# Token loads of a 2:4-pruned matmul: two single tiles instead of a pair on SyncE, and one tile moved to ScalarE's queue

## The chip, the cores and the metric

The kernel runs on one core of a Trainium2 chip. The metric is the device time of one execution in microseconds (us); the number given for a kernel is the median of several runs. Tokens, weights, bias and output are bfloat16.

## The reference

```python
def reference(x, w, b):          # x (16, 512, 1024), w (1024, 1024), b (1024)
    B, S, D = x.shape
    N, M = 2, 4
    G = D // M
    wg = w.reshape(G, M, D)                      # groups of 4 consecutive rows
    mag = jnp.abs(wg)
    order = jnp.argsort(mag, 1)
    thr = jnp.take_along_axis(mag, order[:, M - N:M - N + 1, :], 1)
    mask = (mag >= thr).astype(w.dtype)          # the two largest of four are kept
    wp = (wg * mask).reshape(D, D)
    return jnp.einsum("bsd,df->bsf", x, wp) + b
```

In each column of the weights, of four consecutive rows the two with the larger magnitude are kept and the others are set to zero. Then 8192 tokens are multiplied with the pruned weights, and the bias is added.

## The kernel before

The 8192 tokens are 64 tiles of 128. The weights, 1024 by 1024, are held as four blocks `w_{g}_{h}`: g is the half of the rows, h the half of the columns. A partition of such a block holds four consecutive rows, so that one group of the pruning lies in one partition. The blocks are pruned in six pieces (line 61): four pieces of 256 columns for g = 0, numbers 0 to 3, and two of 512 for g = 1, numbers 4 and 5. `abs_piece` takes magnitudes, `prep_piece` finds the threshold of each group with maxima and minima on VectorE, then the mask (line 150) and the product with the weights (line 153). Piece 0 is done in smaller steps: its product comes first for rows 0 and 1 of the groups in two instructions, then for rows 2 and 3 in one.

TensorE contracts over partitions, so tokens must be transposed. The kernel has three ways:

- Tiles 0 to 7, first half of the contraction: they are loaded as they are (`load_x`, line 79, into tiles `xh`), transposed on TensorE (`transpose_half`, line 182, four 128x128 transposes per tile) into PSUM, and copied to SBUF by ScalarE (`copy_half`, line 187, into `xT`). The transposition gathers every fourth element, so that these tokens meet the weights in the layout in which they are pruned.
- Tiles 0 to 7, second half, and tiles 8 to 13 are loaded by transposing DMAs on SyncE's queue (`xg1`, line 324, and `xfill`, line 259).
- All later tiles are loaded by transposing DMAs, two tiles and then eight at a time (`issue_batch`, line 271).

For all but the first kind the pruned weights are needed in the order of rows; four DMAs per block bring them there (`unpack`, line 172, into `wp_nat`).

In front, the order of the work is written out by hand as a list of short words (`FRONT`, line 285). `W` and `w` are matmuls on constants with which TensorE is kept running until tokens come (line 105); `T.t` transposes tile t; `C.t` copies it; `N.i.t.m` and `M.i.t` multiply tile t with piece i (line 203; 256 columns for pieces 0 to 3); `A` and `P` prune a piece; `U` unpacks; `X` and `Y` are the matmuls of tiles 8 to 13. The words around the change read:

```python
W W W W W W W W W w w T.0 T.1 C.0 T.2 T.3 C.1 w T.4 C.2 N.0.0.0 N.0.0.1
N.0.1.0 N.0.1.1 T.5 N.0.2.0 N.0.2.1 N.0.0.2 N.0.0.3 ...
```

Every engine runs its own instructions in this order and waits at each one for what it needs. The loads stand ahead of this list (lines 83 to 91): each is issued on SyncE's queue or, if `nc.scalar` is named, on ScalarE's. All DMAs of the program, of both queues, take turns on eight completion semaphores; a DMA's issue waits until the one that stands eight places before it has landed.

After the front, TensorE takes one tile after another with 16 matmuls of 512 columns (line 371), VectorE adds the bias (line 248) into a tile `o_pair` that holds the outputs of two tiles, and ScalarE's queue stores it. Pair p holds tiles 2p and 2p + 1; a pair named in `singly` (line 214) is stored in two DMAs, one per tile (lines 221 and 224), the others in one (line 228). There are five such buffers.

Of the kernel before, what the change touches and what calls it, by code (L numbers as in the profile page):

```python
# [10 lines left out]
def kernel(  # L11
# [7 lines left out]
    nc = tc.nc  # L19
# [49 lines left out]
    def load_w(g, c0, c1, eng=nc.sync, m0=0, m1=4):  # L69
        dst = w_gh[(g, c0 // FH)][:, m0:m1, c0 % FH:c0 % FH + c1 - c0]  # L70
        K(eng.dma_start(dst, wv[:, g, m0:m1, c0:c1]))  # L71
# [4 lines left out]
    def load_x(ta, tb, eng=nc.sync):  # L76
        xt = const.tile([P, tb - ta, KH], bf16, name=f"xh_{ta}")
        src = xf[ta * P:tb * P, 0:KH].rearrange("(t p) c -> p t c", p=P)
        K(eng.dma_start(xt[:], src))
        for t in range(ta, tb):  # L80
            xh[t] = xt[:, t - ta, :]

    load_w(0, 0, 256, nc.sync, 0, 2)
    load_w(0, 0, 256, nc.scalar, 2, 4)
    load_x(0, 2)
    load_x(2, 4, nc.scalar)
    load_x(4, 5)
    load_x(5, 6)
    load_w(0, 256, 512)
    load_x(6, 8)  # L90
    load_w(0, 512, 1024)
# [119 lines left out]
            o_left[t // 2] = 2 if t == NT - 2 else 4  # L211
        return o_pair[t // 2][:, t % 2, :]

    singly = range(10, 17)

    def half_done(t):
        p = t // 2
# [188 lines left out]
```

## Time and profile before

| | |
|---|---|
| median of 3 runs | 233.23 us (232.80 to 233.49) |
| the profiled execution's own time | 233.29 us |
| its span in the trace | 231.5 us |
| TensorE busy | 226.3 us, 98% of the span |
| VectorE busy | 120.2 us |
| ScalarE busy | 18.0 us |
| DMA, mean over the span | 165 GB/s |
| first matmul on tokens (a transposition) starts | 5.24 us |
| first matmul with pruned weights starts | 6.44 us |

Times within the trace count from the start of the span. In the profile, PE is TensorE's matmuls and PEld its loading of the stationary operand, DVE is VectorE, ACT is ScalarE, POOL is GpSimd; SPq and ACTq are the instruction queues of SyncE and ScalarE that issue DMAs. A line of the order of time gives the start, the length, engine, source line, operation, output and input, and the number of instructions merged into it; in brackets stands how long the engine was idle before, and what ended that. The length of an issue on SPq or ACTq is the time that the queue needed for it, not the transfer; a transfer's landing is told separately, as the time from issue to landing.

Loads ahead of the front, in their order on each queue, as the trace has them:

| queue | what | size | issued at | issue to landing |
|---|---|---|---|---|
| SyncE | piece 0, rows 0 and 1 of the groups | 128 KB | 0.73 | 2.8 |
| SyncE | tiles 0 and 1 | 256 KB | 1.24 | 4.0 |
| SyncE | tile 4 | 128 KB | 1.75 | 4.2 |
| SyncE | tile 5 | 128 KB | 2.25 | 4.1 |
| SyncE | piece 1 | 256 KB | 2.72 | 4.5 |
| SyncE | tiles 6 and 7 | 256 KB | 3.44 | 4.5 |
| SyncE | pieces 2 and 3 (w_0_1) | 512 KB | 4.09 | 5.9 |
| SyncE | piece 4 (w_1_0) | 512 KB | 4.70 | 6.7 |
| ScalarE | piece 0, rows 2 and 3 of the groups | 128 KB | 0.73 | 3.0 |
| ScalarE | tiles 2 and 3 | 256 KB | 1.25 | 4.4 |

### The profile page before, as it was taken

Reading aid. Unit: us, or ns where it says so; the run is one execution under the profiler, and the core shown is the slowest. Engines: PE = TensorE matmul, PEld = TensorE weight load, DVE = VectorE, ACT = ScalarE, POOL = GpSimd, SP = SyncE. Lnnn points to the kernel's source line nnn. Section 1 sums busy time; section 2 is a strip of 40 time slices with the busy share of each in tenths; the row PEclk is TensorE's granted clock in tenths of the full one; section 3 lists DMA queues with packets and bytes.
Section 4 is the critical chain, followed back from the end, with each engine's and each line's share of the span. In section 5 each row is a group of like instructions: output and inputs, shape, how many; then the busy total and the mean of one; then the engine's idle time right before and its main releaser. Section 6 shows DMA issues by size and latency. Waiting matters only on the chain.

```text
span 231.5 us, 2773 instructions
## 1 busy us (share of the span) xinstructions
PE 226.3 (98%) x1137; PEld 110.5 (48%) x1156; DVE 120.2 (52%) x213; ACT 18.0 (8%) x33; POOL 0.7 (0%) x6
## 2 busy tenths in 40 slices
PE   7999999999999999999999999999999999999995
PEld 3887444444444444444444444444444444444443
DVE  3999887867997324424424424423423433433434
ACT  2867500000000000000000000000000000000000
POOL 1000000000000000000000000000000000000000
PEclk9999999999999999999999999999999999999999
DMA  6999889999647222991249622595128921122222
GB/s 196 295 193 270 192 177 184 267 252 307 258 181 272 91 95 65 233 290 55 84 120 265 159 95 91 131 258 179 69 91 210 316 108 40 53 91 91 91 93 91
DMA packets 77100, 38.19 MB, mean 165 GB/s; under 512 B 63136, under 2 KB 68896, under 8 KB 77088
## 3 DMA queue, kind: packets, MB, share of 16 engines
q1 hardware_dynamic: 67712, 20.91, 42.0%
q10 hardware_dynamic: 9376, 17.11, 20.0%
q8 instruction: 9, 0.15, 0.3%
q14 instruction: 3, 0.02, 0.0%
HBM read 3.41 MB, written 16.78 MB: 87 GB/s over the span
## 4 chain that ended last, share of the span: by engine, by line
PE 96%; DMA 2%; issue 1%; DVE 0%; SPq 0%
PE bank L371 73%; PE bank L203 17%; PE bank L263 6%; DMA xh<-in_x_dram 2%; PE bank L182 1%; DVE o_last L354 0%; SPq L71 0%; PE bank L105 0%
## 5 line engine op out<-in xcount | busy, mean ns | idle before, releaser
L371 PE MATMUL bank<-wp_nat,xTb 128*128 128x512 bf16 x737 | 161.7, 379 | 0.8
L248 DVE TENSOR_TENSOR o_pair<-bank,bias_sb 128x512 bf16<-128x512 f32 x104 | 67.3, 687 | 99.5 <-PE bank L371 94.2
L371 PEld LDWEIGHTS <-xTb 128*128 128x128 bf16 x752 | 73.6, 98 | 88.7
L239 DVE TENSOR_TENSOR stage<-bank,stage 128x512 f32<-128x512 f32 x22 | 14.2, 687 | 4.1 <-PE bank L203 4.1
L203 PE MATMUL bank<-w,xT 128*128 128x256 bf16 x128 | 14.7, 273 | 0.0
L243 DVE TENSOR_TENSOR o_pair<-stage,bias_sb 128x512 bf16<-128x512 f32 x22 | 14.0, 683 | 0.0
L203 PE MATMUL bank<-wp_nat,xg 128*128 128x512 bf16 x62 | 13.9, 379 | 0.1
L203 PEld LDWEIGHTS <-xT 128*128 128x128 bf16 x128 | 12.2, 98 | 1.8 <-ACT xT L187 0.3
L235 ACT COPY stage<-bank 128x512 f32<-128x512 f32 x22 | 11.5, 613 | 4.5 <-PE bank L203 4.5
L203 PE MATMUL bank<-wp_nat,xfill 128*128 128x512 bf16 x47 | 10.6, 379 | 0.1
L263 PE MATMUL bank<-wp_nat,xfill 128*128 128x512 bf16 x47 | 10.5, 379 | 0.1
L203 PEld LDWEIGHTS <-xg 128*128 128x128 bf16 x64 | 6.3, 98 | 7.6
L263 PEld LDWEIGHTS <-xfill 128*128 128x128 bf16 x48 | 4.7, 98 | 5.7
L203 PEld LDWEIGHTS <-xfill 128*128 128x128 bf16 x48 | 4.7, 98 | 5.5
L371 PE MATMUL bank<-wp_nat,xTs 128*128 128x512 bf16 x32 | 7.1, 379 | 0.0
L150 DVE TENSOR_TENSOR mask<-mag,thr 128x512 bf16<-128x512 bf16 (+3 forms) x10 | 5.6, 581 | 0.2
L153 DVE TENSOR_TENSOR w<-w,mask 128x512 bf16<-128x512 bf16 (+3 forms) x10 | 5.6, 580 | 0.1
L371 PEld LDWEIGHTS <-xTs 128*128 128x128 bf16 x32 | 3.1, 98 | 3.8
L105 PE MATMUL bank<-const-bfloat16-1.0 128*128 128x512 bf16 (+1 forms) x12 | 4.0, 493 | 0.8 <-PEq L390 0.8
L187 ACT COPY xT<-bank 128x512 bf16<-128x512 bf16 x8 | 4.1, 605 | 3.0 <-PE bank L182 3.0
L120 DVE TENSOR_SCALAR mag<-w 128x512 uint16<-128x512 uint16 (+2 forms) x6 | 2.7, 466 | 2.8 <-DMA w<-in_w_dram 2.7
L263 PE MATMUL bank<-wp_nat,xTb 128*128 128x64 bf16 (+3 forms) x40 | 3.7, 251 | 0.0
(20 smaller groups left out, 26.1 us busy)
## 6 DMA issues: line engine op xcount, KB each, us to landing
out_dram<-o_pair ACTq DMA_DIRECT2D x24, 512.0 KB, 2.8
out_dram<-o_pair ACTq DMA_DIRECT2D x15, 256.0 KB, 2.0
wp_nat<-w SPq DMA_DIRECT2D x16, 128.0 KB, 2.8
w<-in_w_dram SPq DMA_DIRECT2D x3, 512.0 KB, 5.9
xh<-in_x_dram SPq DMA_DIRECT2D x2, 256.0 KB, 4.2
xh<-in_x_dram ACTq DMA_DIRECT2D x1, 256.0 KB, 4.4
xh<-in_x_dram SPq DMA_DIRECT2D x2, 128.0 KB, 4.2
w<-in_w_dram SPq DMA_DIRECT2D x1, 256.0 KB, 4.5
```

The costliest lines, as they stand in the source:

```text
L105: K(nc.tensor.matmul(bank[7][:, :n], lhsT=ones[:, :P], rhs=ones[:, :n], start=True, stop=True))
L120: K(nc.vector.tensor_single_scalar(mag[:, ms].bitcast(u16), w_of(i)[:, ms].bitcast(u16), 0x7FFF, op=Alu.bitwise_and))
L150: K(nc.vector.tensor_tensor(mask[:, ms, c], mag[:, ms, c], tb, op=Alu.is_ge))
L153: K(nc.vector.tensor_tensor(w_of(i)[:, ms, c], w_of(i)[:, ms, c], mask[:, ms, c], op=Alu.mult))
L187: K(nc.scalar.copy(xt[:], src))
L203: K(nc.tensor.matmul(dst, lhsT=lhs, rhs=rhs, start=c0 == 0 and m == 0, stop=c1 == FH and m == 3))
L235: K(nc.scalar.copy(stage[(h, t)][:], bank[own[(h, t)]][:]))
L239: K(nc.vector.tensor_tensor(st, bank[own[(2 + h, t)]][:], st, op=Alu.add))
L243: K(nc.vector.tensor_tensor(get_o(t)[:, f], stage.pop((h, t))[:], bias_sb[:, f], op=Alu.add))
L248: K(nc.vector.tensor_tensor(get_o(t)[:, f], bank[bk][:], bias_sb[:, f], op=Alu.add))
L263: K(nc.tensor.matmul(bank[bk][:, :c1 - c0], lhsT=xN[t][:, kt, :], rhs=wp_nat[h][:, kt, c0:c1], start=kt == 0, stop=kt == KT - 1))
L371: K(nc.tensor.matmul(bank[bks[h]][:], lhsT=xN[t][:, kt, :], rhs=wp_nat[h][:, kt, :], start=kt == 0, stop=kt == KT - 1))
```

## The change

Tiles 0 and 1 are loaded by one DMA each, both on SyncE's queue, where one DMA brought both. Tile 5 goes from SyncE's queue to ScalarE's, behind tiles 2 and 3. SyncE's queue holds, in this order, the first half of piece 0, tile 0, tile 1, tile 4, piece 1, tiles 6 and 7, and the rest as before. There is one DMA more ahead of the front, so that each later DMA is one place further on in the turn of the eight semaphores. Pair 10, tiles 20 and 21, is no longer in `singly` and is stored by one DMA, so that from there on the turn is as before. The instructions of TensorE, VectorE and GpSimd and their order are the same; on TensorE the first transposition of tile 1 has a wait of its own for its tokens.

```diff
     load_w(0, 0, 256, nc.sync, 0, 2)
     load_w(0, 0, 256, nc.scalar, 2, 4)
-    load_x(0, 2)
+    load_x(0, 1)
     load_x(2, 4, nc.scalar)
+    load_x(1, 2)
+    load_x(5, 6, nc.scalar)
     load_x(4, 5)
-    load_x(5, 6)
     load_w(0, 256, 512)
     load_x(6, 8)
     load_w(0, 512, 1024)
...
-    singly = range(10, 17)
+    singly = range(11, 17)
```

## The prediction

> **What bounds the kernel now.** I read the page's busy shares first, then the chain that ended last, then the order of time of the first 10 us, then SyncE's queue. The profiled execution took 233.29 us, of which 231.5 us are its span; 1.79 us lie around it. The median of the three runs is 233.23 us, so a difference found in the trace is carried over to the median as it is.
>
> ```profile
> PE 226.3 (98%) x1137; PEld 110.5 (48%) x1156; DVE 120.2 (52%) x213; ACT 18.0 (8%) x33; POOL 0.7 (0%) x6
> ```
>
> TensorE is busy for 226.3 of 231.5 us, so only idle TensorE time can be won, and there is little of it. The chain, in order of time (start, length, what), says where:
>
> ```profile
> 1.24 3.96 DMA xh<-in_x_dram
> 5.20 0.05 issue
> 5.24 1.08 PE bank L182 x16
> ...
> 9.46 13.11 PE bank L203 x115
> 22.57 0.05 issue
> 22.62 10.74 PE bank L203 x49
> ```
>
> Up to 5.20 us the end hangs on the first transfer of tokens (tiles 0 and 1, 256 KB, issued at 1.24). From 5.24 on it is TensorE alone; the 0.05 us pieces later on are no wait that the profile can name. So the change can act only in the head. There, in order of time:
>
> ```profile
> 0.77 3.75 PE L105 MATMUL bank<-const-bfloat16-1.0 128*128 128x512 bf16 x11 [0.77 <-PEq L390]
> ...
> 5.24 1.08 PE L182 MATMUL bank<-ident,xh 128*128 128x128 bf16 x16 [0.72 <-DMA xh<-in_x_dram]
> ...
> 5.69 3.04 ACT L187 COPY xT<-bank 128x512 bf16<-128x512 bf16 x6 [2.41 <-PE bank L182]
> 5.88 0.48 DVE L153 TENSOR_TENSOR w<-w,mask 128x256 bf16<-128x256 bf16 x2
> ...
> 6.44 0.77 PE L203 MATMUL bank<-w,xT 128*128 128x256 bf16 x4
> 6.73 0.42 DVE L153 TENSOR_TENSOR w<-w,mask 128x512 bf16<-128x512 bf16 x1
> 6.82 0.11 PEld L203 LDWEIGHTS <-xT 128*128 128x128 bf16 x2 [0.28 <-ACT xT L187]
> ...
> 7.31 1.70 PE L203 MATMUL bank<-w,xT 128*128 128x256 bf16 x14
> ```
>
> The reader is to see four things. TensorE idles 0.72 us (4.52 to 5.24) for the tokens. The first real matmul (6.44) needs the first pruned half of piece 0, and VectorE delivers that at 5.88 + 0.48 = 6.36. The matmuls of tile 1 start at 6.82 because ScalarE's copy of tile 1 ends only then: ScalarE copies one tile every (3.04 - 0.60) / 5 = 0.49 us, and its first copy starts at 5.69. Tile 2's start at 7.31 for the same reason. And the copies begin late only because tile 0's tokens do.
>
> **The change, part by part.**
>
> *Steps of TensorE.* Transposes follow each other by (1.08 - 0.22) / 15 = 0.057 us, so one tile of four takes 0.23; the 256-column matmuls by (1.70 - 0.27) / 13 = 0.11. From a release to the next start I take 0.05 (landing 5.20, start 5.24).
>
> *Tile 0's landing.* Not in the trace as a transfer of 128 KB in the first place. Bounds: at best its half of the pair's bytes is saved at the whole rate of its queue's share. Between 4.5 and 5.24 us the sixteen engines moved about 381 GB/s, two queues at work, so 131 KB at half of that are 0.69 us and at all of it 0.34 us: landing at 4.51 to 4.86; at worst it lands with the pair, at 5.20. I take 4.5, because ScalarE's pair is in flight beside it (landed 1.25 + 4.4 = 5.6). Its four transposes then start at 4.55, right after the warm-up, and ScalarE's first copy at about 4.97 instead of 5.69. Everything up to 5.04 gives the same sum, see the copies below.
>
> *Tile 1's landing.* It has the same bytes ahead of it on its queue as the end of the pair had, so 5.20; the late bound is the slot that it takes over, issued at 1.75, from which tile 4's tokens took 4.2 us: 5.95 to 6.0. I take 5.20, the row of the same bytes. Its transposes run from 5.24, the last ends at 5.63, and its copy starts at 5.66 instead of 6.18.
>
> *Tiles 2 and 3* keep their place (second on ScalarE's queue, landing 5.6): transposes 5.66 to 6.11. One filler matmul, 0.06.
>
> *Tile 4 and tile 5.* Tile 4 stays third of SyncE's token transfers, tile 5 goes to ScalarE's queue. Before, they landed at 5.98 and at 2.25 + 4.1 = 6.38. Now they come side by side: tile 4 at 5.58 at the whole rate of 347 GB/s (window 5.24 to 6.44) counted from 5.20, 5.95 at half, 6.33 at a third; I take 5.95. It is needed at 6.17, so up to 0.1 costs nothing and the late bound costs 0.2. Tile 5 at half rate after 5.62 lands at 6.4 and is needed at 6.85: nothing. The Trainium skill, "DMA: Bandwidth & Descriptors", section "Issuing engines are not separate DMA queues", says that transfers from two engines share the same 16 DMA engines and interleave; it speaks against any gain from spreading, and by it the half-rate figure is the right one, while separate queues would give 5.58. No start on TensorE depends on which.
>
> *First matmul.* Tile 4's transposes end their issue at 6.17 + 0.23 = 6.40, VectorE's half is there at 6.36 + 0.05 = 6.41: first matmul at 6.41 instead of 6.44. Here the next thing that is late shows itself: **VectorE's pruning**. From there two matmuls of tile 0, two of tile 1 (copy done at 5.66 + 0.59 = 6.25, no wait any more), four transposes of tile 5, two matmuls of tile 2 (copy 6.15 to 6.75, no wait): 0.22 + 0.22 + 0.23 + 0.22 = 0.89, so the third matmul of tile 0 starts at 7.30. VectorE's second half is there at 6.73 + 0.42 + 0.05 = 7.20: no wait. Before, that matmul started at 7.31 + 2 x 0.11 = 7.53. **The gain is 0.23 us**, made up of the two waits on ScalarE (0.16 at 6.82, where 6.66 was the next step, and 0.04 at 7.31) and 0.03 at the first matmul. Of the 0.72 us of idle time the rest is only moved, to wait for VectorE. All of it won would be 7.53 - 7.20 = 0.33; more isn't there while VectorE starts at 3.58 with the weights, which the change doesn't touch.
>
> *Is it carried to the end?* Piece 1 is needed by TensorE 14 matmuls after 9.30, at 10.85, now 10.62; VectorE has its first half at 9.94 + 0.42 = 10.36. Slack 0.2 us, and 256 KB of piece 1's weights have the same bytes ahead on their queue. Later pieces have more (pruned at 13.69, used at 14.3). After that no wait stands on TensorE, so the shift reaches the end.
>
> *A new wait on SyncE.* Transfers take turns on eight completion semaphores, and the issue of one waits until the one eight places before it has landed. One more transfer up front moves all later ones by a place. The row that shows such a wait now:
>
> ```profile
> SPq L259 <- DMA xh<-in_x_dram: 0.3, 1, 0.3
> ```
>
> Here the transposing load of xfill waited for tiles 2 and 3 (5.6). After the change it is the transfer before it, the weights of w_1_0, that waits for them: issued at 5.65 instead of 4.70, with 0.63 us of issuing; xfill follows at 6.3 instead of 5.63. Tiles 6 and 7 wait for the first weights (3.55 against an issue at 3.44: 0.1). Behind that on SyncE's queue, each later by 0.7 us at most:
>
> ```profile
> 5.63 6.48 SPq L259 DMA_TRANSPOSE xfill<-in_x_dram  x1
> 12.25 3.50 SPq L172 DMA_DIRECT2D wp_nat<-w  x4
> 15.79 0.62 SPq L71 DMA_DIRECT2D w<-in_w_dram  x1
> 16.46 5.22 SPq L324 DMA_TRANSPOSE xg<-in_x_dram  x1
> 22.48 2.49 SPq L172 DMA_DIRECT2D wp_nat<-w  x4
> ```
>
> Their users: xfill landed at 15.8 and the four unpacks by 17.9, used from 21.2; the last weights at 20.0, used by VectorE at 22.37; xg at 23.8, used at 26.3; the unpacks of 22.48 wait for VectorE's pruning (21.23 + 1.23 = 22.46) and not for the queue, which is free at 21.7, then 22.4. These have the smallest slack: 0.8 us of queue, and 1.2 more from landing (22.48 + 2.6) to use (26.5, now 26.3), 2.0 against 0.7. Cost nothing; without that cover it would be the lateness beyond it, one for one.
>
> *ScalarE's third issue* (0.5 us, row of 1.25) pushes its table load from 1.79 to 2.3, done at 3.8 with the small copy; the first copy is at 4.97. Nothing.
>
> *Output.* Tiles 20 and 21 leave in one store of 512 KB at 84.8 instead of two of 256 KB at 81.34 and 84.79: one issue of 0.35 us less on an idle ScalarE, landing 0.8 later (2.8 against 2.0 us), its buffer used again only five pairs on. Nothing.
>
> Sum: 233.29 - 0.23 = 233.06 against the profiled time, **233.00 us** against the median.
>
> **The rivals.**
>
> 1. *Landing follows the slot, not the bytes.* Then tile 1 lands at 6.0. Transposes of tile 1 at 6.04, tiles 2 and 3, filler and tile 4 behind them (0.95 in all): first matmul at 6.99, third of tile 0 at 6.99 + 0.89 = 7.88 against 7.53: slower by 0.35, 233.6. Decisive from a landing at 5.65 on, where the gain is used up. For it: five SyncE transfers in a row took 4.0 to 4.5 us from issue to landing whatever their size. Against it: DMA engines moved 381 GB/s then, so bytes and not slots were the limit. The Trainium skill, the same page, section "Rules for kernel authors", tells to merge small transfers because each has a fixed cost; by that rule splitting loses.
>
> 2. *Tile 0 isn't earlier.* If the queues share out so that it lands with the old pair (after 5.04), copies start as before and only the 0.03 is left: 233.2. For it: the pair of 256 KB took 4.0 us from its issue and the 128 KB behind it 4.2, so size hardly shows. Against it: those 128 KB were queued behind the pair.
>
> 3. *SyncE's queue becomes the bound.* Only if lateness exceeds 2.0 us; the two xfill loads took 6.48 and 3.29 us to issue for the same size, so 3.2 us of scatter exist, but the longer one is already in the chain. With 3.2 beyond the 0.7, TensorE would wait 1.9 us, less the gain: 1.7 slower, 234.9.
>
> 4. *More than my sum.* Bounded by VectorE at 0.33: 232.9. Over 0.7 us only by something that the profile doesn't show.
>
> **How the numbers follow.** Forecast 0.62 (232.9 to 233.1), rival 2 0.14, rival 1 0.13, rival 3 0.03, rival 4 0.08 (half of it beyond 0.7 us). Within 0.3% (0.70 us), about what a measurement of this kernel can tell from no change, lie the forecast, rival 2 and most of rival 1. The three runs of before scatter from 0.43 below to 0.26 above their median, which puts a few hundredths of each at the bounds: faster 0.09, same 0.83, slower 0.08. The range takes 232.80 - 0.33 = 232.5 below and rival 1 above, 233.6.
>
> **What would show it.** Right: tile 0's transposes start by 4.9; the first matmul at 6.41, directly after VectorE; no wait on ScalarE at tiles 1 and 2; third matmul of tile 0 at 7.30; w_1_0 issued at 5.65; no gap on TensorE at 21 to 27 us. Wrong: tile 1 after 5.65, or a gap on TensorE before tile 4's transposes or tile 5's, or at xfill or xg.

## The result and the profile after

The changed kernel takes 234.58 us, the median of 17 runs (233.55 to 236.29); the kernel before took 233.19 in 17 runs beside them (232.80 to 233.76). The ratio is 1.0069, 95% interval 1.0049 to 1.0088: slower by 1.6 us (the medians lie 1.4 us apart), where 0.2 us of gain were forecast. The profiled execution of after took 233.55 us and is the fastest of its 17; 7 of the 17 took 235.5 us or more.

Busy times are those of before within 0.1 us. From the page of after:

```profile
PE 226.2 (98%) x1137; PEld 110.6 (48%) x1156; DVE 120.2 (52%) x213; ACT 18.1 (8%) x33; POOL 0.7 (0%) x6
```

So the work is the same and the difference is idle time of TensorE. The chain that ended last (start, length, what) says for what:

```profile
1.75 4.16 DMA xh<-in_x_dram
5.95 0.86 PE bank L183 x12
6.81 0.06 PE bank L106
6.87 0.22 PE bank L183 x4
7.09 0.44 PE bank L204 x4
7.53 0.22 PE bank L183 x4
7.75 1.53 PE bank L204 x14
9.28 0.45 PE bank L183 x8
9.72 13.11 PE bank L204 x115
```

Before, the end hung on the tokens issued at 1.24, which landed at 5.20. Now it hangs on the next transfer of the same queue: tile 1, issued at 1.75, landed at 5.90. The way from there to the block of 115 matmuls is shorter than it was: 3.77 us from 5.95 to 9.72, against 4.22 from 5.24 to 9.46. Four transposes, those of tile 0, are already done (0.22 us), and the matmuls that waited for ScalarE's copies no longer wait. In before these two pieces of the chain were:

```profile
6.61 0.61 PE bank L203 x4
...
7.44 1.58 PE bank L203 x14
```

They took 0.44 and 1.53 in after. So 0.71 us were lost at the start and 0.45 won behind it. The 0.26 us that are left are the whole difference between the two profiled executions (233.55 and 233.29). The order of time shows the new wait (in brackets the idle time before, and what ended it):

```profile
0.77 3.87 PE L106 MATMUL bank<-const-bfloat16-1.0 128*128 128x512 bf16 x11 [0.77 <-PEq L391]
...
4.48 0.38 PE L183 MATMUL bank<-ident,xh 128*128 128x128 bf16 x4
...
4.90 0.59 ACT L188 COPY xT<-bank 128x512 bf16<-128x512 bf16 x1 [1.09 <-PE bank L183]
...
5.93 0.49 DVE L154 TENSOR_TENSOR w<-w,mask 128x256 bf16<-128x256 bf16 x2
...
5.95 0.86 PE L183 MATMUL bank<-ident,xh 128*128 128x128 bf16 x12 [1.09 <-DMA xh<-in_x_dram]
...
6.93 0.60 PE L204 MATMUL bank<-w,xT 128*128 128x256 bf16 x4
```

Tile 0 is transposed at 4.48, right after the warm-up, and ScalarE copies it at 4.90. Then TensorE has nothing for 1.09 us until tile 1 has landed. VectorE has the first pruned half at 5.93 + 0.49 = 6.42, but the first matmul starts at 6.93: it isn't VectorE that is late, it is the transposes, which stand ahead of it in TensorE's order. In the waits of after, TensorE has no other wait for data in the whole execution:

```profile
PE bank L183 <- DMA xh<-in_x_dram: 1.1, 1, 1.1
```

That accounts for 233.55. It doesn't yet account for 234.58, the median, nor for the seven runs from 235.5 on.

### The profile page after: what moved, and what is told of

It reads as the page before. It is cut to its first block, busy times and chain, and to the rows that moved or that the text cites. A ratio compares the mean times of both kernels' runs of the same rounds, so it can differ in the third digit from the quotient of the medians.

```text
span 231.8 us, 2771 instructions
## 1 busy us (share of the span) xinstructions
PE 226.2 (98%) x1137; PEld 110.6 (48%) x1156; DVE 120.2 (52%) x213; ACT 18.1 (8%) x33; POOL 0.7 (0%) x6
## 4 chain that ended last, share of the span: by engine, by line
PE 95%; DMA 2%; issue 1%; DVE 0%; SPq 0%
PE bank L372 73%; PE bank L204 16%; PE bank L264 6%; DMA xh<-in_x_dram 2%; PE bank L183 1%; DVE o_last L355 0%; SPq L71 0%; SPq L79 0%; PE bank L106 0%
```

## The experiments

Two questions were open. Why does tile 1 land at 5.90 and not at 5.20? And what makes other runs longer than the profiled one? For the first the theories were: the bytes (what is served ahead, on both queues, sets the landing), the place (the issue slot sets it, whatever the bytes: a queue supplies the engines with one transfer per issue), and short transfers as such, with single DMA engines that come late. For the second: a still later landing, or TensorE's pace after a longer idle time.

A transfer counts as landed when sixteen completions are in. They are taken here as one for each of the sixteen DMA engines, though the trace names no engine. Where landings are told below, they are read from the trace: first, twelfth and last of the sixteen.

### Which part of the change costs

**e1_split_only**: the changed kernel, with tile 5 left on SyncE's queue.

```diff
-    load_x(5, 6, nc.scalar)
     load_x(4, 5)
+    load_x(5, 6)
```

> Only the split of tiles 0 and 1 is done; tile 5 stays on SyncE's queue behind tile 4. Theory of turns (the DMA engines serve one transfer of SyncE's queue, then one of ScalarE's, and so on, so tile 1 stands behind the 256 KB of tiles 2 and 3): the split alone is what delays tile 1, which lands at about 5.9 as in the changed kernel, with tile 4 next at about 6.2 and tile 5 at 6.6; the first matmul with weights starts at about 6.9, the third of tile 0 at 7.8 against 7.53 before. Rival, contention with tile 5 on ScalarE's queue delays tile 1: then tile 1 lands at 5.2 here and the time is 233.0. Time by turns: 233.5 at the least, and as far up as 236 in some runs if the longer idle time of TensorE brings its clock down.

**e2_move_only**: the kernel before, with only tile 5 moved to ScalarE's queue.

```diff
     load_x(0, 2)
     load_x(2, 4, nc.scalar)
+    load_x(5, 6, nc.scalar)
     load_x(4, 5)
-    load_x(5, 6)
```

> Only tile 5 goes to ScalarE's queue, tiles 0 and 1 stay one transfer of 256 KB. If the split alone is the cause (as the run with the split alone suggests: 234.2 with tile 5 on SyncE's queue), nothing changes: tiles 0 and 1 land at 4.6 to 5.2, time 233.2 within 0.2. Rival, the move is a cause of its own (short transfers on two queues at once hold some of the 16 DMA engines up): tile 4 or tile 5 lands after 6.5 and TensorE waits for it; 233.5 or more.

Measured: the split alone 234.20 (233.63 to 234.64, 7 runs; before 233.21), ratio 1.0039 [1.0025, 1.0052], tile 1 landed at 5.99. The move alone 233.21 (232.96 to 234.05, 10 runs; before 233.11), ratio 1.0004 [0.9993, 1.0015]. The split costs; moving tile 5 costs nothing that can be measured. On the chip of e1_split_only the whole change cost no more than the split alone (e7_after_again, below: 1.0031).

### The place in the queue, or the bytes

**e17_third_slot**: the kernel before, with the pair of tiles kept, but SyncE's half of piece 0 in two transfers of 64 KB. The pair has the same bytes ahead of it and is third instead of second.

```diff
-    load_w(0, 0, 256, nc.sync, 0, 2)
+    load_w(0, 0, 256, nc.sync, 0, 1)
+    load_w(0, 0, 256, nc.sync, 1, 2)
...
-    singly = range(10, 17)
+    singly = range(11, 17)
```

> Before, with SyncE's half of piece 0 in two transfers of 64 KB: tiles 0 and 1 stay one transfer of 256 KB with the same bytes ahead of it, but it is the third in SyncE's order, issued at about 1.75 instead of 1.24. If the landing goes by the place in the queue and its issue, the pair lands where the third transfer lands elsewhere, 5.5 to 6.8 us (in before 5.98); the third matmul of tile 0 comes that much later than at 7.53, 0.3 to 1.6, so 233.5 to 234.8 us, and longer where TensorE loses its pace. If it goes by the bytes ahead, the pair lands at 4.6 to 5.2 as in before, and the time is 233.0 to 233.4 us. If short transfers as such make some engines late, the last of the sixteen completions comes 0.7 us or more behind the twelfth; else within 0.4 us as in before.

Measured: 235.29 us (234.36 to 236.12, 6 runs; before 233.12), ratio 1.0086 [1.0060, 1.0111]. The chain of e17_third_slot begins:

```profile
1.18 0.42 SPq L71
1.65 4.46 DMA xh<-in_x_dram
6.15 1.90 PE bank L183 x16
```

The pair, whole and with no byte more ahead of it on its queue, was issued at 1.65 and landed at 6.10. In before it landed at 5.20, in e2_move_only, e4_less_warm and e10_no_warm, where it is second too, at 4.58 to 5.02. So the bytes ahead on its own queue, by which it had to come at 4.6 to 5.2, don't set the landing. But it isn't the start that is late. The first completion came at 4.58 (4.67 in before), the twelfth at 5.44 (4.94), the last at 6.10: the spread grew from 0.53 to 1.52 us. The last came 0.66 us behind the twelfth, between the two bounds that the expectation had set for short transfers as such. And the other queue isn't held fixed: ScalarE's tiles 2 and 3, which had landed behind the pair in before (5.62), landed ahead of it here (5.16). The lengths show a second loss, taken up further down: sixteen transposes took 1.90 us where before took 1.08.

**e18_act_short_first**: the changed kernel, with ScalarE's queue in the order tile 5, then tiles 2 and 3, so that half as many bytes are served between tile 0 and tile 1.

```diff
-    load_x(2, 4, nc.scalar)
+    load_x(5, 6, nc.scalar)
     load_x(1, 2)
-    load_x(5, 6, nc.scalar)
+    load_x(2, 4, nc.scalar)
```

> The changed kernel with ScalarE's queue in the order tile 5, then tiles 2 and 3: tile 1 keeps its place and issue (third on SyncE, 1.75), but the transfer that the queues serve between tile 0 and tile 1 has 128 KB instead of 256. If tile 1 is late because of the bytes served in between, its first completions come at about 4.4 instead of 4.75 and its last by 5.3; tiles 2 and 3 come last, at 5.6 to 6.0, and the time is 233.2 to 233.8 us. If it is late by its place in the queue, its last completion stays at 5.9 to 6.7 and the time is 234.0 to 235.

Measured: 234.75 us (234.68 to 236.50, 4 runs; before 233.12), ratio 1.0089 [1.0054, 1.0124]. Tile 1's first completion came at 4.61 instead of 4.75, its last at 6.31; tiles 2 and 3 landed only at 7.33, and TensorE waited for both. What the DMA engines did meanwhile is shown by stretches of 0.5 us. A line holds each engine's busy time, then the granted clock, the DMA share (the mean busy share of the sixteen DMA engines; overlapping packets can bring it over 1) and GB/s. In e18_act_short_first:

```profile
4.00:4.50 0.50, 0.50 (x2) 0.15 (x1) 0.50 (x3) 0.00 (x0) 0.00 (x0) 1.00 0.23 59
4.50:5.00 0.50, 0.50 (x6) 0.43 (x5) 0.50 (x4) 0.00 (x0) 0.00 (x0) 1.00 0.63 223
```

The same stretches of before, where the pair and tiles 2 and 3, 512 KB, filled them:

```profile
4.00:4.50 0.50, 0.50 (x4) 0.20 (x2) 0.50 (x4) 0.00 (x0) 0.00 (x0) 1.00 1.02 361
4.50:5.00 0.50, 0.03 (x1) 0.00 (x0) 0.50 (x3) 0.00 (x0) 0.00 (x0) 1.00 1.09 381
```

And those of after:

```profile
4.00:4.50 0.50, 0.50 (x5) 0.24 (x4) 0.50 (x4) 0.00 (x0) 0.00 (x0) 1.00 1.13 256
4.50:5.00 0.50, 0.36 (x7) 0.20 (x4) 0.50 (x4) 0.10 (x1) 0.00 (x0) 1.00 0.73 248
```

And the first of them in e5_act_singles (further down), where tiles 2 and 3 are split too:

```profile
4.00:4.50 0.50, 0.50 (x2) 0.15 (x1) 0.50 (x3) 0.24 (x2) 0.00 (x0) 1.00 1.05 373
```

The last two columns are to be read. In e18_act_short_first hardly a byte moved at 4.0 to 4.5 us. Tile 1 had been issued at 1.75 and tile 4 at 2.21, and all ahead of them had landed by 4.34. A reading that fits is that the engines had nothing to work on yet: an issue of 128 KB (1.75 to 2.21, 0.46 us) takes SyncE about as long as one of 256 KB (1.24 to 1.75, 0.51 us in before), so that two short transfers give the engines in two slots what one pair gives them in one. At 4.0 to 4.5 us eleven of the thirteen profiles with tiles 0 and 1 split moved 59 to 320 GB/s, and the four that have the pair where before has it (before, e2_move_only, e4_less_warm, e10_no_warm) moved 346 to 381. But the reading isn't shown. In after the share was 1.13 while 256 GB/s were moved: the engines were busy, and some packets took long, up to 0.89 us where most took 0.05. And e5_act_singles, which has the most short transfers in front, moved 373.

**The same question from other sides.** Each is the changed kernel with one edit; e5_act_singles, e12_pool, e13_w_sp_split and e14_w_sp_pair shift `singly` by the DMA that they add or take away, as the change does.

```diff
e6_x1_act: tile 1 on ScalarE's queue, tiles 2 and 3 third on SyncE's
-    load_x(2, 4, nc.scalar)
-    load_x(1, 2)
+    load_x(1, 2, nc.scalar)
+    load_x(2, 4)

e5_act_singles: tiles 2 and 3 in two transfers too
-    load_x(2, 4, nc.scalar)
+    load_x(2, 3, nc.scalar)
     load_x(1, 2)
+    load_x(3, 4, nc.scalar)

e8_one_queue: all tokens on SyncE's queue
-    load_x(2, 4, nc.scalar)
     load_x(1, 2)
-    load_x(5, 6, nc.scalar)
+    load_x(2, 4)
     load_x(4, 5)
+    load_x(5, 6)

e11_w_on_act: SyncE starts with tile 0
-    load_w(0, 0, 256, nc.sync, 0, 2)
+    load_w(0, 0, 256, nc.scalar, 0, 2)

e12_pool: tile 1 issued by GpSimd
-    load_x(1, 2)
+    load_x(1, 2, nc.gpsimd)

e13_w_sp_split: piece 0 whole on SyncE, ScalarE starts with tiles 2 and 3
-    load_w(0, 0, 256, nc.sync, 0, 2)
-    load_w(0, 0, 256, nc.scalar, 2, 4)
+    load_w(0, 0, 256)

e14_w_sp_pair: as e13_w_sp_split, with tiles 0 and 1 in one transfer again
-    load_x(0, 1)
+    load_x(0, 2)
     load_x(2, 4, nc.scalar)
-    load_x(1, 2)
```

> Tile 1 alone goes to ScalarE's queue and tiles 2 and 3 to SyncE's, so that by turns the order is tile 0, tile 1, tiles 2 and 3, tile 5, tile 4. Theory of turns alone: tile 1 lands at 4.4 to 4.9, tiles 2 and 3 at 5.4, TensorE has no wait but that for VectorE's pruning, first matmul with weights at 6.4 or sooner if the weights land sooner; 233.0. Rival, stragglers: tile 1 is early, but tiles 2 and 3 now take the late place and land at 5.9 to 6.6; 233.4 to 234.2.

> The changed kernel with tiles 2 and 3 as two transfers of 128 KB on ScalarE's queue too, so that tile 1 stands behind 128 KB of that queue and not 256 (one transfer more in the turn of the semaphores, tiles 22 and 23 stored by one DMA to make up for it). Theory of turns alone: tile 1 lands 0.35 to 0.7 us sooner than in the changed kernel, at 5.2 to 5.5; time 233.0 to 233.2. Rival, stragglers: in the changed kernel most of the sixteen completions of tile 1's transfer come by 5.3 and the last ones 0.6 to 1.3 us later, because short transfers let the engines drift apart; with still more short transfers the last completion comes no sooner, 5.9 to 6.7, and the time is 233.8 or more.

> The same transfers as with the split, but all tokens on SyncE's queue in the order 0, 1, 2 and 3, 4, 5; ScalarE's queue has only its half of piece 0. If two queues at work beside each other make the last completions late, they come close together here (within 0.5 us of the first), tile 1 lands by 4.9, tiles 2 and 3 by 5.7: 233.0 to 233.2. If short transfers do it by themselves, the last completions of tile 1 are 0.6 us or more behind the first here too, and TensorE waits for tile 1 or for tiles 2 and 3: 233.5 or more.

> The changed kernel with the first half of piece 0 issued on ScalarE's queue too, so that tile 0 is SyncE's first transfer, tile 1 its second and tile 4 its third. Theory of the slot (SyncE's third transfer gets its last completions late whatever it carries; tile 1 is third in the changed kernel, tile 4 in the kernel before): tile 1 has its sixteen completions within 0.5 us and before 4.9, and tile 4 is the one with late ones. Rival, the transfer that follows a short one is late: tile 1 is spread over 0.7 us or more here too. The weights of piece 0 come up to 0.5 us later, so the time itself tells little: 233.2 to 233.9.

> The changed kernel with tile 1 issued from GpSimd, a third queue, and tile 4 as SyncE's third transfer (singly as in the kernel before, since GpSimd's transfers have semaphores of their own). Theory of the slot: tile 1 lands together on all engines, by 5.3, tile 4 has late completions; TensorE may wait for tile 4, 233.0 to 233.6. Rival, engines drift apart because many short transfers are in flight: tile 1 late on some engines here too, 233.8 or more. GpSimd's own cost of issuing is unknown: if it takes 2 us more, tile 1 lands after 6 on all engines alike.

> The changed kernel, but piece 0 comes by one transfer of 256 KB ahead on SyncE's queue and ScalarE's queue starts with tiles 2 and 3; tiles 0 and 1 stay split. They then follow 0.8 us of transfers on either queue instead of 0.4. Theory of supply (tile 1's late engines come from its descriptors reaching some engines only after these have used up the short transfer of tile 0): tile 1's sixteen completions lie within 0.6 us and TensorE doesn't wait long; 232.9 to 233.3. Rival, late engines come with short transfers as such: tile 1 is spread over 1 us or more, 233.5 or more.

> As the run with piece 0 in one transfer on SyncE's queue, tile 5 on ScalarE's queue too, but tiles 0 and 1 as one transfer of 256 KB. The split is the only difference between the two. If the split costs by itself, this one is 0.3 to 1 us faster than that one; if it only costs where the queue has little ahead of it, the two are equal, or this one is up to 0.25 slower since tile 0 comes later.

| run | median us (range, runs) | ratio to before, 95% interval | tile 1 lands | third transfer on SyncE |
|---|---|---|---|---|
| e6_x1_act | 233.96 (233.84 to 234.25, 5) | 1.0034 [1.0020, 1.0047] | 4.50 | tiles 2, 3: 4.67 first, 6.54 last |
| e5_act_singles | 233.58 (232.92 to 234.54, 10) | 1.0024 [1.0007, 1.0041] | 5.11 | tile 1: 4.64, 5.11 |
| e8_one_queue | 234.80 (234.50 to 235.34, 4) | 1.0070 [1.0051, 1.0089] | 5.42 | tile 1: 4.25, 5.42 |
| e11_w_on_act | 233.74 (233.67 to 234.70, 9) | 1.0032 [1.0021, 1.0042] | 4.03 | tile 4: 4.21, 5.45 |
| e12_pool | 233.50 (233.22 to 233.94, 10) | 1.0012 [1.0003, 1.0020] | 5.99 | tile 4: 5.10, 6.72 |
| e13_w_sp_split | 234.80 (234.72 to 234.85, 5) | 1.0071 [1.0059, 1.0083] | 5.98 | tile 1, issued at 2.13: 5.13, 5.98 |
| e14_w_sp_pair | 235.53 (234.61 to 237.47, 6) | 1.0110 [1.0075, 1.0146] | 6.82 | tile 4, issued at 2.13: 5.70, 7.23 |

What follows from them:

- In e6_x1_act tile 1 is the second transfer of ScalarE's queue, and it landed at 4.50; now tiles 2 and 3, put into the third place on SyncE, came at 6.54 and were what TensorE waited for. Here the lateness stays with the place and not with the tile.
- Over the kernels in which SyncE's third transfer was issued at 1.65 to 1.76, seventeen profiles, it landed at 5.11 to 6.76, with 128 KB ahead of it on its queue (e17_third_slot), 256 KB or 384 KB (before: 5.98). The second, where it was tile 0, tile 1 or the pair, landed at 3.87 to 5.20. In before the third is tile 4, which isn't needed until 6.17.
- The place doesn't settle it, though. In e5_act_singles tile 1 is third, issued at 1.74, and it landed at 5.11, even a little before the 5.2 to 5.5 of the theory of turns; the median, 233.58 us, lies between the two forecasts. In e14_w_sp_pair the pair is second, issued at 1.48, and it landed at 6.82. In e12_pool tile 1 stands alone on a third queue, issued at 1.24, and it landed at 5.99, where the theory of the slot had 5.3.
- Nor do the bytes that are served in between. e5_act_singles and e18_act_short_first both have 128 KB there in place of 256; the first completions of tile 1 agree (4.64 and 4.61), but the last lie 1.2 us apart (5.11 and 6.31).
- Two queues side by side aren't needed for it: in e8_one_queue, with all tokens on SyncE's queue, tile 1's completions still lay 1.17 us apart (4.25 and 5.42).
- Short transfers as such don't settle it either. In e11_w_on_act tile 1, second behind a short one, was spread over 0.73 us (3.30 to 4.03), just over the 0.7 that the expectation had set for it, and tile 4, third, over 1.24; in e13_w_sp_split tile 1 was spread over 0.85, between the two bounds. But e5_act_singles has only short transfers of tokens there and a spread of 0.47, and in e14_w_sp_pair the pair, 256 KB, has fifteen of its completions by 5.82 and the last at 6.82. That kernel was 0.7 us slower than e13_w_sp_split, where the expectation had at most 0.25.
- No other order of the queues wins. e8_one_queue pushed the later loads back, and TensorE waited 1.5 us for tiles 6 and 7, landed at 10.8. In e13_w_sp_split piece 0 lands at 5.28 instead of 3.55, and the chain runs through VectorE's pruning.

So what is shown is that the split makes the last completions late: with ScalarE's queue as in the change, tile 1 landed at 5.90 to 6.76 in six profiles, and the pair at 4.58 to 5.20 in the four that have it where before has it. Why they are late stays open. In nine of the profiles with the split the first completion of SyncE's third transfer came at 4.61 to 4.81; the others are e8_one_queue (4.25), e11_w_on_act (4.21), e12_pool (5.10) and e13_w_sp_split (5.13). In after the twelfth of tile 1 came at 5.22, about where the forecast had all sixteen; a few came later, the last at 5.90, in other runs of the same kernel at 6.6. Which engines they are and what holds them isn't in the trace, and no experiment settled it. There is one profile of each kernel, and e5_act_singles, with runs from 232.92 to 234.54, shows how much one kernel varies.

### Runs longer than the profiled one

**e7_after_again** and **e9_after_third**: the changed kernel again, unchanged, for more profiles.

> The changed kernel as it is, beside the others on one chip. Theory of turns: order of landing tile 0, tiles 2 and 3, tile 1, tile 5, tile 4; tile 1 at about 5.9 in every profile. Theory of the clock: runs from 233.5 to 236.3; if the profiled one is long, its matmuls with 256 columns take 0.22 us from one to the next for a stretch after 5.9 us where they took 0.11. Rival, late transfers: the profile of a long run has a wait of TensorE for a transfer instead.

> The changed kernel a third time, since its first runs reached 236.3 and its second ones only 234.3. Theory of the late engines: the time is 233.2 plus the lateness of tile 1's last completion over about 5.65, so 233.5 to 234.4, with granted clock 1. Theory that the clock takes part: some runs at 235.5 or more, with a granted clock of 0.993 in some of them, on chips where tile 1 lands still later.

Measured: 234.03 us (233.78 to 234.30, 6 runs), ratio 1.0031 [1.0019, 1.0043], and 234.38 (233.73 to 236.32, 7 runs), ratio 1.0064 [1.0036, 1.0092]. The two profiled executions took 234.30 and 235.66 us. TensorE in order of time, e7_after_again:

```profile
4.59 0.39 PE L183 MATMUL bank<-ident,xh 128*128 128x128 bf16 x4
6.70 0.86 PE L183 MATMUL bank<-ident,xh 128*128 128x128 bf16 x12 [1.72 <-DMA xh<-in_x_dram]
...
7.67 0.60 PE L204 MATMUL bank<-w,xT 128*128 128x256 bf16 x4
```

And e9_after_third:

```profile
4.78 0.63 PE L183 MATMUL bank<-ident,xh 128*128 128x128 bf16 x4
6.69 1.47 PE L183 MATMUL bank<-ident,xh 128*128 128x128 bf16 x12 [1.28 <-DMA xh<-in_x_dram]
...
8.48 1.06 PE L204 MATMUL bank<-w,xT 128*128 128x256 bf16 x4
```

Same kernel, same landing of tile 1 (6.65 and 6.64), and yet the third matmul of tile 0 starts at 8.55 in the one and at 9.92 in the other. Read the lengths: twelve transposes took 0.86 us and 1.47. In e9_after_third each started 0.11 us after the one before, in e7_after_again 0.056. So there are two terms. The landing, 6.65 against 5.20 in before, made e7_after_again slower by 8.55 - 7.54 = 1.01 us, and its execution by 234.30 - 233.29 = 1.01. The slow pace made e9_after_third slower by another 9.92 - 8.55 = 1.37; its execution was longer by 1.36.

**e10_no_warm**: the kernel before without the warm-up matmuls, to price a slow start. **e4_less_warm**: with one of them fewer, to lengthen the idle time a little.

```diff
- ... A.0 P.0 W W W W W W W W W w w T.0 T.1 ...
+ ... A.0 P.0 w T.0 T.1 ...                        (e10_no_warm)
+ ... A.0 P.0 W W W W W W W W w w T.0 T.1 ...      (e4_less_warm)
```

> The kernel before without the matmuls on constants ahead of the tokens (one short one is left), transfers unchanged. It prices TensorE at its slow pace: if the transposes and matmuls that follow 5.2 us run at half pace for about 3.4 us, as the constants do in their first 3.2 us now (0.43 us from one to the next, later 0.22), the time is 233.2 + 1.7 = 234.9. Rival, the pace at the start costs nothing because VectorE and the transfers are the limit there: 233.2 to 233.6.

> The kernel before with one matmul on constants fewer ahead of the tokens, so that TensorE idles about 1.1 us instead of 0.72 before the first transposition; no transfer is changed. Theory of the clock: the runs scatter as those of the changed kernel do, some of them 1 to 3 us over 233.2, with granted clocks under 1 in some. Rival, the scatter comes from the transfers: all runs lie within 232.8 to 233.8.

Measured: e10_no_warm 234.62 us (234.22 to 235.13, 4 runs), ratio 1.0064 [1.0050, 1.0078]; in its profile the transposes start 0.11 us apart until about 7.2. A cold start of TensorE costs about 1.4 us here, the size of the second term. e4_less_warm: 233.22 (232.96 to 233.73, 11 runs), ratio 0.9997 [0.9987, 1.0008]. All its runs lie where the rival had them, but it doesn't decide about the idle time, since in its profile the pair happened to land at 4.58, and nearly no idle time was left to look at.

**e3_fill** and, once more, **e16_fill_again**: the changed kernel, with five of the constant matmuls put between the transposes of tile 0 and of tile 1, so that TensorE is busy for most of the wait.

```diff
- ... W W w w T.0 T.1 C.0 ...
+ ... W W w w T.0 W W W W W T.1 C.0 ...
```

> The changed kernel with five more matmuls on constants of 512 columns between the transposes of tile 0 and those of tile 1, that is 5 x 0.216 = 1.08 us of TensorE work in the idle time of 1.09 us. Nothing else differs, tile 1 lands as late as before. Theory of the clock (the scatter of the changed kernel, 233.55 to 236.29, comes from TensorE running at half rate for a while because of the longer idle time): the scatter goes and all runs lie near 233.5, which is the 233.2 of before and the 0.27 that tile 1's late landing costs. Rival, the scatter comes from transfers that land at different times from run to run: it stays, with a median near 234.5.

> The changed kernel with five more constant matmuls between the transposes of tiles 0 and 1, once more. Of 30 runs of the changed kernel 10 took 235.5 us or more, and the profile of one of them has TensorE at half pace from 6.7 to 9.7 us. Theory of the idle time (TensorE's full pace is granted only after about 3.4 us of work without a long gap; a warm-up that ends before the grant and then idles for over a microsecond loses it): with the gap filled no run reaches 235.4, median 234.3 or less. Rival, the grant comes at random whatever TensorE does: about a third of the runs at 235.5 or more here too.

Measured: 234.34 us (234.28 to 234.73, 5 runs), ratio 1.0048 [1.0034, 1.0061], and 234.37 (234.23 to 234.82, 5 runs), ratio 1.0056 [1.0043, 1.0070]. Tile 1 landed at 6.64 and 6.76 in their profiles, and the transposes behind ran at the quick pace. So filling doesn't take the lateness away, as it must not. But none of ten filled runs took over 234.82 us, whereas of thirty runs of the changed kernel nine took 235.5 or more (the expectation above counts ten; the runs on record show nine). That speaks for the idle time as what lets the pace stay slow, but weakly. With nine long runs among forty, all nine would fall outside ten given ones about 5 times in 100. And the runs come from several chips: on the one where both kernels ran side by side (e3_fill and e7_after_again) neither had a run of 235.5.

## Why the prediction was wrong

**What failed** is the step "Tile 1's landing": "It has the same bytes ahead of it on its queue as the end of the pair had, so 5.20". It landed at 5.90 in the profile, and at 6.64 and 6.65 in two more of the same kernel. The step had two faults. It counted the bytes on SyncE's queue alone; but in before the pair landed ahead of ScalarE's tiles 2 and 3 (5.20 and 5.62), and in after tile 1 landed behind them (5.17 and 5.90). And it took over one landing where there are sixteen completions: twelve were in at 5.22, about when all were forecast, but the spread from first to last had grown from 0.53 to 1.15 us.

The late bound that stood beside it, 5.95 to 6.0, from the row of the third SyncE transfer, came nearest, and so did the landing of rival 1, "Landing follows the slot, not the bytes", with a chance of 0.13. Its sum holds: first matmul 6.99 (measured 6.93), third of tile 0 at 7.88 (7.80), 233.6 us (233.55 profiled). That it meets the profile so well is in part luck, since this execution is the fastest of its 17, and the experiments did not bear out its mechanism alone: SyncE's third transfer landed anywhere from 5.11 to 6.76. Rival 1 was set aside because "DMA engines moved 381 GB/s then, so bytes and not slots were the limit". That rate was a property of the order with the pair: in after it was 256 and 248 GB/s at 4 to 5 us. A rate read in the old kernel needn't hold in a new one with other transfers. For the place spoke that "five SyncE transfers in a row took 4.0 to 4.5 us from issue to landing whatever their size", and that should have weighed more.

The Trainium skill, "DMA: Bandwidth & Descriptors", section "Rules for kernel authors", tells to merge many small transfers into one large one and names 64 KB as the size below which overhead prevails. The direction agrees, though the tiles here have 128 KB: e1_split_only loses 0.39%. The same page, section "Queues, rings and completion order", says that a DMA engine serves the queues in turn, a packet of some 9 to 17 descriptors each. The order of landing in after agrees (tile 0, tiles 2 and 3, tile 1, tile 5, tile 4: SyncE, ScalarE, SyncE, ScalarE, SyncE); but e18_act_short_first, where the turn in between was half as long, brought the first completion 0.14 us forward and the last not at all (6.31), and e5_act_singles, with the same turn, brought the last to 5.11.

**What was missing** is that rival 1 has a tail. The range ended at a landing of 6.0. In five profiles more of kernels with tile 0 and tile 1 split on SyncE and tiles 2 and 3 as a pair on ScalarE it was 5.99 (e1_split_only), 6.64, 6.65, 6.64 and 6.76. What lay beyond rival 1's turning point of 5.65 was paid one for one: 0.25 us in after (0.26 lost), 1.00 in e7_after_again (1.01).

**A term that wasn't in the sum** is TensorE's pace. The prediction counted idle time as moved, not as harmful. But the idle time between tile 0 and tile 1 grew to 1.1 to 1.7 us, and where the constants had ended at the slow pace, TensorE could stay slow: 1.4 us in e9_after_third, and the 1.90 us of e17_third_slot. It didn't always: in e12_pool, e14_w_sp_pair and e18_act_short_first the constants ended slow too (4.98), and the transposes after idle times of 0.61, 1.88 and 0.95 us were quick. The Trainium skill, "TensorE: Matmul & The Clock Gate", section "What's actually happening", says that TensorE runs at half its clock until it was busy for a window of about 3.4 us, and that this window runs freely and doesn't start with the kernel. The traces agree in the two paces (0.107 and 0.056 us per transpose) and in that the moment differs from run to run: the eleven constants ended at 4.64 in after, quickened at the last, and at 4.98 in e9_after_third, all slow. That runs of 235.5 us and more are long for this reason was seen in one profile of the changed kernel only, that of e9_after_third; none of the seven among the 17 was profiled.

**What was right:**

- Tile 0 comes early: 4.05, even before the bound of 4.51; transposed at 4.48 and copied at 4.90, forecast at 4.55 and 4.97. It gains nothing, since tile 1 stands behind it in TensorE's order ahead of the first matmul.
- The gain that was looked for exists at the front. In the profile of e2_move_only the pair happened to land at 4.78; its third matmul of tile 0 started at 7.33 instead of 7.54, and that execution took 233.08 us instead of 233.29: 0.21 us, where the forecast had 0.23. The bound by VectorE exists too. In e5_act_singles, where tile 1 landed at 5.11, the first matmul started at 6.33, just behind VectorE's first half (5.79 + 0.48 = 6.27), and the third of tile 0 at 7.21, the whole 0.33 that the prediction had as the most.
- The new wait on SyncE came and cost nothing in after. w_1_0 was issued at 5.19, when tiles 2 and 3 had landed (5.17, earlier than thought, so it wasn't 5.65), and xfill at 5.78 instead of 5.63. Tiles 6 and 7 waited for ScalarE's half of piece 0 (3.79) and not for SyncE's (3.61). In SyncE's queue, after:

```profile
3.81 0.39 SPq L79 DMA_DIRECT2D xh<-in_x_dram  x1
4.24 1.49 SPq L71 DMA_DIRECT2D w<-in_w_dram  x2
5.78 6.63 SPq L260 DMA_TRANSPOSE xfill<-in_x_dram  x1
```

- ScalarE's third issue put its table load to 2.31 (forecast 2.3) and cost nothing, nor did the joined store of tiles 20 and 21: the waits of TensorE name neither.

**What else didn't hold** is the step "Is it carried to the end?", "no wait stands on TensorE, so the shift reaches the end". The two profiles with the earliest fronts gave their lead back at the unpacked weights, the `wp_nat` that the prediction had with the smallest slack:

```profile
PE bank L203 <- DMA wp_nat<-w: 0.4, 1, 0.4
PE bank L205 <- DMA wp_nat<-w: 0.3, 1, 0.3
```

The first line is of e4_less_warm (third matmul of tile 0 at 7.13, 0.41 us ahead of before), the second of e5_act_singles. The unpacks were issued at 24.06 and 23.74 where before issued them at 22.48, since the transposing loads ahead of them in SyncE's queue took longer to issue: 7.70 us for xfill in e4_less_warm, 6.63 for xg in e5_act_singles, against 6.48 and 5.22. TensorE stood still at 26.9 and 26.7, and the two executions took 233.73 and 233.44 us, longer than before. This is the prediction's rival 3, and in e4_less_warm it comes without any change of the transfers. So even tile 1 at 5.20 would have been no sure gain.

## What to carry to other kernels

When a change puts a transfer one place further back in a queue, take the row of that place as a bound that may well come true, and not the row of the same bytes alone; look also at what the other queue then gets served first. A transfer has landed with the last of its sixteen completions, and the spread from first to last can grow with the order of the transfers: a forecast needs that spread and not one landing. A DMA rate read in the old order needn't hold in a new one. Before splitting a load so that its first part comes early, look for what needs the second part, and whether anything can be done in between. And a lead won early counts only if the next wait behind it has room for it.

## What the runs showed of the hardware

- The sixteen DMA engines moved only 59 GB/s for half a microsecond (e18_act_short_first, 4.0 to 4.5 us) while transfers issued about 2 us earlier were still to be served. From issue to the first of sixteen completions, SyncE's third transfer took 2.5 us (e8_one_queue, e11_w_on_act) to 3.7 (tile 4 in before).
- The sixteen completions of one transfer can lie far apart: 0.53 us for the pair in before, 1.15 us for tile 1 in after, 1.95 in e16_fill_again, where fifteen were in by 5.20 and the last at 6.76.
- Half pace of TensorE isn't always in the record of the granted clock. The profile of e9_after_third gives a mean granted clock of 1.000 with transposes 0.11 us apart up to 8.4; four of the seven runs of after from 235.5 us on show 0.993, the other three 1.000.
